# A gated mix of attention and a ReGLU block on one core: early weight loads merged in pairs, the last chunk of x moved to a later place, and the order of work laid out anew

## The chip, the cores and the metric

The kernel runs on one NeuronCore of one Trainium2 chip, as one program. The metric is the device time in microseconds of one execution; lower is better. All times of the trace are microseconds from the span's start, unless a row says ns.

## The reference

The input `x` has 2048 tokens of 512 numbers in bf16. Two branches work on it and a gate per token mixes them.

```python
g = sigmoid((x * gate_w).sum(-1, keepdims=True))
return g * A(x) + (1 - g) * B(x)
# B: three projections, D = 512, F = 1792
gate = x @ W_gate; up = x @ W_up
B = (gate * (gate > 0) * up) @ W_down
# A: 32 heads of 16, four segments of 512 tokens, a memory M, z carried from one to the next
for s in range(4):
    logits = qs @ ks.T * scale + mask      # mask: key after query
    a_dot = softmax(logits) @ vs
    a_mem = (phi(qs) @ M) / (phi(qs) @ z + 1e-6)
    o = sig(beta) * a_mem + (1 - sig(beta)) * a_dot
    M = M + phi(ks).T @ vs; z = z + phi(ks).sum(tokens)
A = o @ wo                                  # phi(t) = t + 1 if t > 0 else exp(t)
```

## The kernel before, in words

Everything is written out as a list of single steps, and each step goes to one engine's program in a fixed order. A step is a group of matmuls, one instruction of VectorE, ScalarE or GpSimd, or one transfer that SP issues. The string `ORDER` has one letter for each step to come; a letter stands for one of the queues that are made at the end of `program` (such as score blocks, exponentials, projections, the ReGLU block, the loads), and each letter takes that queue's next step. `BANKS` names the accumulator of each group in the same way. `Sched.place` derives the semaphore waits from what a step reads and writes. The numbers `occ`, `nbytes` and `after` given with a step are the planner's costs and due times; they went into the making of `ORDER` and set nothing on the chip. A transfer is tied to one of 16 semaphores, and an issue waits until the last transfer on its semaphore has landed.

Work is staged by four segments (chunks) of 512 tokens. For each there are:

- `proj` (L538 to L573): q, k and v by TensorE, in pairs of contraction tiles (`kt`, four of 128 rows), copied out by VectorE or ScalarE (L552, L556, L560, L573); masked copies `kp` of k (L564, L565); `phi` of q and k (L525 to L527), and a transpose of phi(k) by a transfer (L570, `phik`).
- `att` (L648): 18 score blocks ("quads") of a segment in the four banks `psL`, the exponential on ScalarE (L652), triangular masks on GpSimd (L657), then the product with v (L680, 64 matmuls a block), which also reads `vsh`, a copy of v shifted by 64 partitions (L630). VectorE transposes and scales the result (L690 to L707). The memory's part is L590 (update), L610 and L617 to L622 (use).
- `ffn` (L740): 14 slices of W_gate and W_up, the relu (L748, L749) and the product into `hT` (L751).
- `outp` (L772, L779): output of the segment before, scaled (L788, L789) and stored (L791).
- the token gate: rows of x are loaded into one buffer (L494, `ldxr4` to `ldxr15`), multiplied and summed by VectorE (L497, `gate4` to `gate15`), one after the other. The first four (L489) use the rows already loaded for chunk 0. `gexp` is written out and read back as `gexpT` (L505, L507).

The matmuls of score blocks, of L680 and L590 and of all the rest run in different array shapes, and TensorE runs its steps in order; so a step that waits holds all steps behind it. The ReGLU block and the output fill the time between score blocks.

All loads go through SP in the order of its letters: four pieces of x (chunk 0), `wq`, `wk`, `wv` in pieces of 128 rows, the first half (`load_gu(0)`) of W_gate and W_up in pieces of 128 rows and 896 columns, `braw` (beta), `gwb` (gate_w), the second half, then chunk 1 of x by four transposing transfers (L383). Chunks 2 and 3 of x and `wo` and W_down have queues of their own and stand where ORDER has put them. In the new file the lines up to this place are one less (L353 for L354).

Of the kernel before, what the change touches and what calls it, by code (L numbers as in the profile page):

```python
# [21 lines left out]

LETTERS = "abcdefghijklmnopqrstuvwxyzABCDEFGHIJKLMNOPQRSTUVWXYZ0123456789"
ORDER = (
    "gefafafefafefafefaefaggfgagggggahgihaisggsagggssaghgssigsahssissasbsssassssassssCassssBsasssCsasBabsasEsasHaEHsasyIaDpasaIwsIasDasaFsaysSIapsaFSwauIau"
    "FasLubSsIapjFSuwSukaunuLSuKSapnuwukuLSVuSLuVSuSndpKuwnuduLSuSuLSduKSkpRmuwkdsLSuSRsosBKSUsSsmREsnUSpJIsBlwusRuDUssxSLpSqUBSwSIsozsuzJSpSsDwSsdzSuIsBds"
    "KSpIsEQdswSQuuduFSsSLysScpzqFSwsPuzqcLToySzpTuSzwsSczuTsSFuTxuSLcsSLpSGsSzwsRszcBsuzsEpRswnUuuBSuSUIuKpIuzSwouSLsSsSLsSEQuuQKpsSRwuBSuuSLqKSRypuzSUSwu"
    "zuSUsLuzuSKnpuwsIoLSuSsDSuJSszpLSCuSwzsusQuLSuESnpKqzwSoszVsVzuGuSzuSyLpSszSwzsusFszuKSuSFpStnwLtSrtOumOSmopOStwSnWtItIuSrLtSpSOtOwSotOSMtqSWSpzswtXzs"
    "ztFrtSOpztOSwzttoOStSzWNSrtSOxpOSXtOStwIWtIsQttRxpSRswtBStSMsSuQXpntwAosQuuDSuStLSKqSRpUqPSRuUwzStTuzTUuTLuSpzKuTUnwtuzoSuzuuLKSpuSzwSuLStSuIuLJSpSsnw"
    "stAosBSsSuQEpSLtwSuSMuuXLuSqnLmSpmouSwzuSuzunsLSpuzSwLSuSsIosBuKSszuJzsEuLSSszuSCrApKuOOwuOuuLuLuSpSLqwuzVuVzuSKsSzpSzuwzsuSDuuLKSpzuSwSsAsLSWssFSpGrS"  # L30
    "ItwOSIttOStOStopSrWSwtSOtOtOtMWStSprXwuOtOtuOtxSLpWSqSwQtzSutzxSuSnpswsLSosSFtuzNSuIpJXLSuSwuzuQuLSuLsSpzGqwtnPSotzTqTQpzSuwTtzStSAttnptzSwouzzttSMTuz"
    "XStSKpAuwLSuStntuLSmpJSoIuwuSLtStSuStmSLrStOSunoNOpOuwuLuuXLruSOuOSKpOSuwSuLuqLSpSzuwSuzSuLuuzKSpzuwzuuLSSuzuSKpSAqwLSuzVuVzuSKpSzuwSzuLSuuzuKpSzuSwLu"
    "SuSAuuLWSuLSuKSuWSpLuwutLtStSrpSOtOwSuOtWtuSpLtSwttMtXSpuSwStSttqSSpSztwStzuztLtNSztzXtrSzuStOSOptOwtWuqLSpSzuwuztLuuzSpztwztMSSuAXuuzSKpStAwtSLtSuSuL"
    "SuSuKSuSpLuwuuLutLSuSuSuKSpuwuLtuqLSSpzuwuzuLuuzKSuzuzuuLSKSpzuSwuAtLuuLSuSvLSpuSwtuMuuLXSuSuLSvKSuvvuvLquzuzvKvzvzuzvuzvLvvAvvvvNvXNvvXvvvvvvNvvvXvvv"
    "vvvvNvvvvvXMX"
)
# [281 lines left out]
def program(sc, nc, T, PL, PA, A_x, A_wq, A_wk, A_wv, A_wo, A_beta, W_g, W_u, W_d, gate_w, out, NSEG, KT, NF, NT, EPS, SCALE):  # L318
    V = type("V", (), T)

    def op(eng, fn, occ, **k):
        return sc.add(Op([(eng, fn, occ)], **k))
# [30 lines left out]
    def load(eng, names, dst, src, nbytes, occ=460.0):  # L353
        (lact if eng == "act" else lsp).append(dma(eng, lambda e, dst=dst, src=src: e.dma_start(dst, src), nbytes, occ=occ, writes=names, name="ld" + names[0]))  # L354
    x0 = A_x[0, 0:512, :].rearrange("(i p) d -> p i d", p=128)
    def touch(n, src):
        load("act", ["adT"], V.adT[0:16, 32 * n:32 * n + 32], src, 1024)
    def load_x0(i):
        load("sp", [f"hT{i}"], V.hT[:, i, :], x0[:, i, :], 150000)

    def load_w(nm, w, src, kts):
        for kt in kts:
            load("sp", [f"{nm}{kt}"], w[:, kt, :], src[kt * 128:(kt + 1) * 128, :], 160000)
    load_x0(0)
    load_x0(1)
    load_w("wq", V.wq, A_wq, (0,))
    load_x0(2)
    load_x0(3)
# [12 lines left out]
    def load_x(c):
        for kt in range(KT):
            lsp.append(dma("sp", lambda e, c=c, kt=kt: e.dma_start_transpose(V.xT[:, kt, c * 512:(c + 1) * 512], A_x[0, c * 512:(c + 1) * 512, kt * 128:(kt + 1) * 128]),  # L383
                           1 << 17, occ=1280.0, writes=[f"xT{c}_{kt}"], name=f"ldx{c}_{kt}"))
# [57 lines left out]
    for h in range(2):  # L442
# [5 lines left out]
        for kt in range(KT):  # L448
            src, dst = PL[:, kt, 0:256], V.xT[:, kt, 256 * h:256 * h + 256]
# [78 lines left out]

    def proj(s):
        pes, evs, sbs, acts, sps = [], [], [], [], []  # L530
# [20 lines left out]
        def cp(fn, **k):  # L551
            return sc.add(Op([("dve", lambda e: fn(e, e.tensor_copy), t_dve(512)), ("act", lambda e: fn(e, lambda d, x: e.activation(d, x, ACT.Copy)), t_act(512))], **k))  # L552
        for G in range(4):
            ep = pj(V.wq, G, "q", "wq")
            qs = qslot(s, G)
            evs.append(cp(lambda e, f, ep=ep, qs=qs: f(V.qT[:, qs, :], A(ep)[:, :]), writes=[f"qT{qs}"], name=f"qcp{s}_{G}", ep=ep, role="r"))  # L556
            if s > 0 and G % 2:
                phi(s, "q", G, V.phiq, "phiq", V.qT, qs - 1, [f"qT{qs - 1}", f"qT{qs}"], acts, sbs)
            ep = pj(V.wk, G, "k", "wk")
            evs.append(cp(lambda e, f, ep=ep, G=G: f(V.kT[:, G, :], A(ep)[:, :]), writes=[f"kT{G}"], name=f"kcp{s}_{G}", ep=ep, role="r"))  # L560
            ks = kslot(s, G)
            kv = V.kT[:, G, :].rearrange("q (c k) -> q c k", c=8)
            for p in range(2):
                km = lambda e, kv=kv, p=p, ks=ks: e.tensor_scalar(V.kp[:, ks, :, 64 * p:64 * p + 64], kv, V.pm[:, p:p + 1], None, ALU.mult)  # L564
                ka = lambda e, kv=kv, p=p, ks=ks: e.activation(V.kp[:, ks, :, 64 * p:64 * p + 64], kv, ACT.Copy, scale=V.pm[:, p:p + 1])  # L565
                evs.append(sc.add(Op([("dve", km, 350)] + ([("act", ka, 720)] if s else []), reads=[f"kT{G}", "pm"], writes=[f"kp{ks}_{p}"], name=f"kmask{s}_{G}_{p}")))
            if s < NSEG - 1 and G % 2:
                phi(s, "k", G, V.ek, "ek", V.kT, G - 1, [f"kT{G - 1}", f"kT{G}"], acts, sbs)
                for g in (G - 1, G):
                    sps.append(dma("sp", lambda e, g=g: e.dma_start_transpose(V.phik[:, :, g * 128:(g + 1) * 128], V.ek[:, g, :]), 1 << 17, occ=1280.0, reads=[f"ek{g}"], writes=[f"phik{g}"], name=f"kT2{s}_{g}"))  # L570
# [320 lines left out]
```

## Time and profile before

| what | value |
|---|---|
| times of the runs | 265.28, 265.44 and 331.41 us; median 265.44 us |
| the profiled execution | 265.18 us, of it the span 263.2 us |
| TensorE busy | 259.5 us (99%), 2761 matmuls, clock 1.000 |
| VectorE busy | 189.3 us (72%), 365 instructions |
| ScalarE busy | 186.4 us (71%), 162 instructions |
| GpSimd busy | 124.7 us (47%), 283 instructions |
| transfers | 19.34 MB, mean 73 GB/s over the span |

The span goes from the first to the last instruction; the profiled execution's own time has 1.98 us more around it. The busy share of an engine is a mean over the whole span. The rows of a timeline give the start, the duration of the group, the engine (SPq is SP's queue of transfer issues), the line, the operation, the tiles written and read, the count and, in brackets, how long the engine stood idle before and what ended that. The row of a transfer issue lasts as long as SP is busy with it; when the data has landed is told by the view of transfers, as the median time from issue to landing.

### The profile page before, as it was taken

What the parts mean: (1) busy time and instruction counts of PE and PEld (TensorE: products, weight loads), DVE (VectorE), ACT (ScalarE), POOL (GpSimd) and SP (SyncE); (2) the same over time, 40 slices, a digit from 0 to 9 for tenths busy, and PEclk for the clock granted to TensorE, in tenths of its full rate; (3) what the DMA queues carried; (4) which work ended last, traced back from release to release, by engine and by line L of the source; (5) the groups of instructions that cost most, each with busy time, mean ns of one, the idle gap of its engine ahead of it and who ended that gap; (6) DMA issues with size and microseconds to landing.
All of it is one profiled execution on the core that took longest, in us unless ns stands there. A gap on an engine that the chain in (4) does not pass through costs nothing.

```text
span 263.2 us, 6640 instructions
## 1 busy us (share of the span) xinstructions
PE 259.5 (99%) x2761; PEld 115.2 (44%) x2761; DVE 189.3 (72%) x365; ACT 186.4 (71%) x162; POOL 124.7 (47%) x283
## 2 busy tenths in 40 slices
PE   8999999999999999999999999999999999999996
PEld 4644444334444444334444434444443443444444
DVE  5588887877887778888896779778854676485700
ACT  3688899888987694887686886868866567664021
POOL 3037456654645456755345467635554526334000
DMA  6889764693041222501032210110321010000011
GB/s 181 259 315 218 163 73 64 188 288 48 21 108 21 63 62 60 83 27 17 2 85 62 64 40 24 38 25 2 85 42 40 22 22 20 0 2 20 2 40 40
DMA packets 34684, 19.34 MB, mean 73 GB/s; under 512 B 24032, under 2 KB 34144, under 8 KB 34656
## 3 DMA queue, kind: packets, MB, share of 16 engines
q1 hardware_dynamic: 34560, 18.93, 31.0%
q8 instruction: 21, 0.34, 0.6%
q14 instruction: 7, 0.06, 0.1%
q10 hardware_dynamic: 96, 0.00, 0.0%
HBM read 9.87 MB, written 2.11 MB: 46 GB/s over the span
## 4 chain that ended last, share of the span: by engine, by line
PE 90%; SPq 4%; DVE 2%; DMA 2%; issue 0%; DVEq 0%
PE psA L740 35%; PE psA L779 19%; PE psL L648 8%; PE psA L547 7%; PE psA L680 6%; PE psA L772 5%; PE psA L545 4%; SPq L383 2%; DMA osb<-in_A_x_dram 2%; PE psA L538 2%; PE psA L610 1%; PE psL L437 1%; SPq L507 1%; SPq L570 1%; PE psL L446 1%; DVE Tn L690 0%
## 5 line engine op out<-in xcount | busy, mean ns | idle before, releaser
L657 POOL TENSOR_SCALAR_AFFINE_SELECT E<-E 64x256 bf16<-64x256 bf16 (+1 forms) x256 | 116.0, 464 | 114.6 <-ACT E L652 105.9
L652 ACT ACTIVATE E<-psL 128x2048 bf16<-128x2048 f32 x72 | 135.1, 1876 | 35.2 <-PE psL L648 32.9
L740 PE MATMUL psA<-xT,wu 128*128 128x512 bf16 x224 | 62.5, 380 | 0.0
L740 PE MATMUL psA<-xT,wg 128*128 128x512 bf16 x224 | 60.8, 380 | 0.0
L779 PE MATMUL psA<-wd,hT 128*128 128x512 bf16 (+2 forms) x238 | 59.3, 367 | 0.0
L751 DVE TENSOR_TENSOR hT<-psA,rl 128x512 bf16<-128x512 f32 x56 | 38.3, 687 | 14.6 <-PE psA L740 13.1
L779 PEld LDWEIGHTS psA<-wd,hT 128*128 128x128 bf16 x238 | 21.4, 98 | 24.1 <-issue 2.8
L740 PEld LDWEIGHTS psA<-xT,wg 128*128 128x128 bf16 x224 | 20.5, 98 | 25.3 <-issue 1.9
L740 PEld LDWEIGHTS psA<-xT,wu 128*128 128x128 bf16 x224 | 20.0, 98 | 25.6 <-issue 4.3
L690 DVE STREAM_TRANSPOSE Tn<-psA 128x512 f32<-128x512 f32 x32 | 21.0, 694 | 12.4 <-PE psA L680 12.4
L748 ACT ACTIVATE rl<-psA 128x512 bf16<-128x512 f32 x32 | 19.1, 596 | 14.5 <-PE psA L740 14.5
L648 PE MATMUL psL<-qT,kp 32*128 32x192 bf16 (+7 forms) x512 | 28.5, 287 | 0.0
L749 DVE TENSOR_SCALAR rl<-psA 128x512 bf16<-128x512 f32 x24 | 16.5, 688 | 6.8 <-PE psA L740 6.6
L648 PEld LDWEIGHTS psL<-qT,kp 32*128 32x128 bf16 x512 | 8.2, 92 | 26.3 <-issue 12.7
L680 PE MATMUL psA<-E,vaug 64*17 64x128 bf16 (+7 forms) x512 | 18.7, 283 | 0.0
L680 PE MATMUL psA<-E,vsh 64*17 64x128 bf16 (+7 forms) x512 | 18.3, 283 | 0.0
L547 PE MATMUL psA<-xT,wk 128*128 128x512 bf16 x64 | 17.1, 380 | 0.0
L545 PE MATMUL psA<-wv,xT 128*128 128x512 bf16 x64 | 16.8, 380 | 0.0
L772 PE MATMUL psA<-wo,oT 128*128 128x512 bf16 (+2 forms) x68 | 16.5, 367 | 0.0
L788 DVE TENSOR_SCALAR osb<-psA,omg 128x512 bf16<-128x512 f32 (+1 forms) x9 | 6.3, 705 | 13.6 <-PE psA L772 10.7
L680 PEld LDWEIGHTS psA<-E,vaug 64*17 64x17 bf16 x512 | 11.6, 86 | 7.8 <-issue 3.4
L789 ACT ACTIVATE osb<-psA,omg 128x512 bf16<-128x512 f32 (+1 forms) x8 | 5.4, 673 | 12.1 <-PE psA L772 10.7
(72 smaller groups left out, 237.0 us busy)
## 6 DMA issues: line engine op xcount, KB each, us to landing
vsh<-vaug SPq DMA_DIRECT2D x8, 272.0 KB, 3.7
out_dram<-osb SPq DMA_DIRECT2D x15, 128.0 KB, 1.7
wg<-in_B_W_gate_dram SPq DMA_DIRECT2D x8, 224.0 KB, 6.4
wu<-in_B_W_up_dram SPq DMA_DIRECT2D x8, 224.0 KB, 6.0
wd<-in_B_W_down_dram SPq DMA_DIRECT2D x3, 512.0 KB, 6.4
osb<-in_A_x_dram SPq DMA_DIRECT2D x12, 128.0 KB, 2.2
hT<-in_A_x_dram SPq DMA_DIRECT2D x4, 128.0 KB, 2.2
wq<-in_A_wq_dram SPq DMA_DIRECT2D x4, 128.0 KB, 2.8
```

What stands on the lines that cost most here:

```text
L545: ins = e.matmul(A(ep)[:, :], lhsT=V.xT[:, kt, tok + col * 128:tok + (col + 1) * 128], rhs=w[:, kt, :], start=(kt == 0), stop=(kt == KT - 1))
L547: ins = e.matmul(A(ep)[:, :], lhsT=w[:, kt, col * 128:(col + 1) * 128], rhs=V.xT[:, kt, tok:tok + 512], start=(kt == 0), stop=(kt == KT - 1))
L648: ins = q.matmul(PL[:, jj, o:o + 512 - 64 * c], lhsT=V.kp[r, kslot(s, G), c, :], rhs=V.qT[r, qslot(s, G), 64 * c:512], start=True, stop=Tr ...
L652: acts.append(act(lambda a: a.activation(V.E[:, e, :, :], PL[:, :, :], ACT.Exp, scale=SCALE), t_act(2048), reads=[f"bankL{b}" for b in ran ...
L657: pools.append(pool(lambda g, ap=ap, base=base: g.affine_select(out=ap, in_=ap, compare_op=ALU.is_ge, fill=0.0, base=base, pattern=[[0, 4] ...
L680: ins = q.matmul(A(eps[p])[32 * jj:32 * jj + 17, 64 * c:512], lhsT=v[:, 8 * G + 2 * jj + p, :], rhs=V.E[r, e, jj, o:o + 512 - 64 * c], sta ...
L690: ds.append(dve(lambda e, p=p, ep=eps[p]: e.transpose(V.Tn[:, p, :], A(ep)[:, :]), 706, writes=[f"Tn{p}"], name=f"tr{s}_{G}_{p}", ep=eps[p ...
L740: ins = e.matmul(A(ep)[:, :], lhsT=w[:, kt, f * 128:(f + 1) * 128], rhs=V.xT[:, kt, c * 512:(c + 1) * 512], start=(kt == 0), stop=(kt == K ...
L748: evs.append(sc.add(Op([("act", lambda e, ep=eg, r=r: e.activation(V.rl[:, r, :], A(ep)[:, :], ACT.Relu), t_act(512)), ("dve", lambda e, e ...
L751: evs.append(dve(lambda e, ep=eu, r=r, hs=hs: e.tensor_tensor(V.hT[:, hs, :], A(ep)[:, :], V.rl[:, r, :], ALU.mult), t_dve(512), reads=[f" ...
L772: ins = e.matmul(A(ep)[:, 0:c1 - c0], lhsT=V.oT[:, o0 + G, i * 128:(i + 1) * 128], rhs=V.wo[:, G, c0:c1], start=st_ and G == 0, stop=sp_ a ...
L779: ins = e.matmul(A(ep)[:, 0:c1 - c0], lhsT=V.hT[:, slots[f], i * 128:(i + 1) * 128], rhs=V.wd[:, f, c0:c1], start=st_ and f == f0, stop=sp ...
```

## The change

The merged loads, and the place of the last chunk:

```diff
-    def load_x0(i):
-        load("sp", [f"hT{i}"], V.hT[:, i, :], x0[:, i, :], 150000)
-
-    def load_w(nm, w, src, kts):
-        for kt in kts:
-            load("sp", [f"{nm}{kt}"], w[:, kt, :], src[kt * 128:(kt + 1) * 128, :], 160000)
...
-    load_w("wq", V.wq, A_wq, (1, 2, 3))
-    load_w("wk", V.wk, A_wk, range(KT))
-    load_w("wv", V.wv, A_wv, range(KT))
+    def load_x0(i, nb):
+        load("sp", [f"hT{i}"], V.hT[:, i, :], x0[:, i, :], nb)
+
+    def load_w(nm, w, src, k0, k1, nb, a=0, b=512, tag=""):
+        load("sp", [f"{nm}{tag}{kt}" for kt in range(k0, k1)], w[:, k0:k1, a:b], src[k0 * 128:k1 * 128, a:b].rearrange("(k p) c -> p k c", p=128), nb)
...
+    load_w("wq", V.wq, A_wq, 1, 2, 250000)
+    load_w("wq", V.wq, A_wq, 2, 4, 280000)
+    load_w("wk", V.wk, A_wk, 0, 2, 440000)
+    load_w("wk", V.wk, A_wk, 2, 4, 280000)
+    load_w("wv", V.wv, A_wv, 0, 4, 780000)
...
-            for kt in range(KT):
-                load("sp", [f"{nm}{h}_{kt}"], w[:, kt, a:b], src[kt * 128:(kt + 1) * 128, a:b], 256 * (b - a) + (748000 if (nm, h, kt) == ("wg", 0, 0) else 0))
+            for kt in (0, 2):
+                load_w(nm, w, src, kt, kt + 2, 410000 + (200000 if (nm, h) == ("wg", 0) else 0), a, b, f"{h}_")
...
-                           1 << 17, occ=1280.0, writes=[f"xT{c}_{kt}"], name=f"ldx{c}_{kt}"))
+                           1 << 17, occ=1350.0, writes=[f"xT{c}_{kt}"], name=f"ldx{c}_{kt}"))
...
-    load("sp", ["braw"], V.braw[:], A_beta.partition_broadcast(128), 8192)
-    load("sp", ["gwb"], V.gwb[:], gate_w.partition_broadcast(128), 400000)
+    load("sp", ["braw"], V.braw[:], A_beta.partition_broadcast(128), 300000, occ=670.0)
+    load("sp", ["gwb"], V.gwb[:], gate_w.partition_broadcast(128), 500000)
...
-            t.after = 22000.0 + 14000.0 * (c - 2)
+            t.after = (24000.0, 100000.0)[c - 2]
```

The planner's cost of a phik transpose goes from 1280 to 1450. `ORDER` (1499 letters, 1513 before, for 14 loads fewer) and `BANKS` are other strings: the same steps in another order and in other accumulators, and for steps that two engines can do, another choice between VectorE and ScalarE in some places. What follows from that on SP: 20 loads stand ahead of chunk 1 where there were 34; two phik transposes now come between chunk 1 and `vsh`; chunk 3, which stood ahead of `wo`, now stands behind the third store of segment 0 and the load `ldxr9`, with two phik transposes between its third and its fourth piece.

More of the change, by code (lines that the diff above doesn't have):

```diff
@@ L24 @@
 ORDER = (
[L25 to L32, printed above, removed]
@@ L33 @@
-    "SuSAuuLWSuLSuKSuWSpLuwutLtStSrpSOtOwSuOtWtuSpLtSwttMtXSpuSwStSttqSSpSztwStzuztLtNSztzXtrSzuStOSOptOwtWuqLSpSzuwuztLuuzSpztwztMSSuAXuuzSKpStAwtSLtSuSuL"
-    "SuSuKSuSpLuwuuLutLSuSuSuKSpuwuLtuqLSSpzuwuzuLuuzKSuzuzuuLSKSpzuSwuAtLuuLSuSvLSpuSwtuMuuLXSuSuLSvKSuvvuvLquzuzvKvzvzuzvuzvLvvAvvvvNvXNvvXvvvvvvNvvvXvvv"
-    "vvvvNvvvvvXMX"
+    "gefafafefafefafefaefaggfgagggggahgihaigagggggsashsisggasshissassbssassssassssssasCssssaBssssCassBasasEassHEHsasyIDpsIwsaIsDuFsaysSIsFSubpIsKIsRwuFuRuu"
+    "LUjSuKkpnuwUksLSuSuFuSKSpnVuwVuLSuSunduKpnuwLSduSukSsLSudblkpmsLSwSsdRsBuSSsoDmpSsSnwIuBSsuLsJSuRqELSUxSpIswzSuUuzssLoCuSIsyzuSDpSsSwLsIsBusIxsQpDSuSw"
@@ new lines @@
+    "QsucFsSuSLypSszLScuwouFqzqcPKSzTpuSzwSuzTscSuLTuzSsKRpscFSwuSzuRusLSUuSGzpsKUIswIunuBSosSuLTsSpzEuSQwuLSuSsQssLCSpSsRwsDSssRqCnUyQpuzSUwSszSssSDuozuSK"
+    "zpszwsBSuSuDSuJSzpuSwLSuSuLuIuLKSuSpynqLwouVzuVuzsKSzpSszwszuFSuSsLSpGuSzwSsLtSnrsOmStOmoGpSOtSwnWtSIsIsrFtSpSOtOwSotOSttMSpWtSwttXrtOtOSpOSuwSWtStqMo"
+    "SXpSztwSzStItzrItxOSpztOSztwtOuStSzWtxSMSpqQXwtPunuLTouKSudRtLSqSdApRtwdzStTuzTuUTunKpuwzSuUQtLSuSuzdKpQuwIuoLSuSuIuLSpStzwutLSuSMuSKpSnXuwuLsSouSzqSK"
+    "SRpzSuwSszSuBsuLSsSuzEnpuKIsIwuAuzLSuSszKssCRsmDSsUmsSCzSrsSOUpnEOuAwuOuouLuLuSpQqwLSuzVuVzsSKuSozpSzswzuuBSusLKSpzuSwSsAuDSWssLSpGrSItwOSIttOStOStWpS"
@@ new lines @@
+    "tSwrStoOtOtONSWtSprwtXOuOtOutWxSLpSqSwQuzSttzxSsSnptwtIoMStSzXtIuzQpuLSwsSzutFSuKSunutLSoqSzptwPtAtQqMTSpXTztSwzStTnusKztSozuzupSztTwLuSsSAutFSKtSntum"
+    "SpmouSnwIuLSuuIuLSptLSwSuMSuosLrsSOuOSGpOXuwuLuuLruSOpOSuLwSuSOuuLqSLSpSzuwSuzuLuuzSuLSuKzpzuwuSzuSLuuLSpqSAwLuVzuVuSKzuSpSzuLwSuzuzuuLSpzuSwSuLSuAuLu"
+    "WSpKLuSSwuWStLuuSrKtSOStOtSOptwWtuurLtSpSOtOwtOMtWtSpqSXwSStzuztSuSzpSKztzwttSztMtStAXpStwStStuqSSpztwtztMuzXSpztwzuuLSSuLuSpSztSwLuStSAutLSuSuSuLSuuK"
+    "upLuwuuLtuSpLuSwSuSuLtuSuLSpuwuLuuLtSuNSuLSuXSuLpqwuzuLuSpSzvwSvLSuzuzuzKuSuzuSLuSKuSAvqLvzvzvvzuzvzuuzKuAvLvvvvvvvNvXNvvXvvvvvvNvvvXvvvvvvvNvvvvvXMX"
@@ L36 @@
 )
 BANKS = (
-    "012312301230123012301320132013201320312032012031023123013201320130231023102301313120101312302302302320323201320132012012301230132030203013013023021010"
-    "21313012012301230123012301230131230302012012320320320320320320321321321310"
+    "012312301230132032013201320123012310231032102310213201320123013021320123012310212120231223130130130130123013021302302301230123012013101201230130320313"
+    "01301301201230123012301203120320202013013232012012012012013203120120120203"
 )
@@ L357, in touch @@
         load("act", ["adT"], V.adT[0:16, 32 * n:32 * n + 32], src, 1024)
-    def load_x0(i):
-        load("sp", [f"hT{i}"], V.hT[:, i, :], x0[:, i, :], 150000)
-    def load_w(nm, w, src, kts):
-        for kt in kts:
-            load("sp", [f"{nm}{kt}"], w[:, kt, :], src[kt * 128:(kt + 1) * 128, :], 160000)
[L364 to L368, printed above, removed]
-    load_w("wq", V.wq, A_wq, (1, 2, 3))
-    load_w("wk", V.wk, A_wk, range(KT))
-    load_w("wv", V.wv, A_wv, range(KT))
+    def load_x0(i, nb):
+        load("sp", [f"hT{i}"], V.hT[:, i, :], x0[:, i, :], nb)
+    def load_w(nm, w, src, k0, k1, nb, a=0, b=512, tag=""):
+        load("sp", [f"{nm}{tag}{kt}" for kt in range(k0, k1)], w[:, k0:k1, a:b], src[k0 * 128:k1 * 128, a:b].rearrange("(k p) c -> p k c", p=128), nb)
+    load_x0(0, 150000)
+    load_x0(1, 150000)
+    load_w("wq", V.wq, A_wq, 0, 1, 250000)
+    load_x0(2, 130000)
+    load_x0(3, 130000)
+    load_w("wq", V.wq, A_wq, 1, 2, 250000)
[3 more added lines that the diff above has]
+    load_w("wv", V.wv, A_wv, 0, 4, 780000)
     half = (NF // 2) * 128
@@ L569, in proj @@
                 for g in (G - 1, G):
-                    sps.append(dma("sp", lambda e, g=g: e.dma_start_transpose(V.phik[:, :, g * 128:(g + 1) * 128], V.ek[:, g, :]), 1 << 17, occ=1280.0, reads=[f"ek{g}"], writes=[f"phik{g}"], name=f"kT2{s}_{g}"))
+                    sps.append(dma("sp", lambda e, g=g: e.dma_start_transpose(V.phik[:, :, g * 128:(g + 1) * 128], V.ek[:, g, :]), 1 << 17, occ=1450.0, reads=[f"ek{g}"], writes=[f"phik{g}"], name=f"kT2{s}_{g}"))
         for tt in range(4):
```

## The prediction

> **What bounds the kernel now.** I read the page's totals first, then the waits of TensorE, then the timeline round the one wait, last the queue that issues the transfers.
>
> ```profile
> span 263.2 us, 6640 instructions
> PE 259.5 (99%) x2761; PEld 115.2 (44%) x2761; DVE 189.3 (72%) x365; ACT 186.4 (71%) x162; POOL 124.7 (47%) x283
> ...
> 13.36 2.16 PE psA L545 x10
> ...
> PE psL L437 <- PEq L876: 0.8, 1, 0.8
> PE psA L547 <- DVE hT L751: 0.4, 1, 0.4
> ```
>
> TensorE is busy for 99% of the span, and its waits name only the start and one stall. A busy figure can hide gaps, since the ends are modelled, so I laid the matmuls of the old order end to end: 0.216 us for each of 512 columns (the chain's row: ten in 2.16). With 0.43 us for a score block, 1.10 for a block of L680 and the change-over before it, the sum meets the starts of all score blocks in the trace within 0.1 us, once two things are added: some 1.3 us in the head, and one step of 0.6 us near 57 us. So after the head the old kernel loses 0.6 us in all. The rest is work.
>
> ```profile
> 56.22 1.03 PE L547 MATMUL psA<-xT,wk 128*128 128x512 bf16 x4
> 57.67 0.60 PE L547 MATMUL psA<-xT,wq 128*128 128x512 bf16 x2 [0.42 <-DVE hT L751]
> ...
> 54.42 0.69 DVE L497 CUSTOM_DVE_ANT_0 osb<-osb,gwb 128x512 bf16<-128x512 bf16 x1 [1.56 <-DMA osb<-in_A_x_dram]
> ...
> 56.97 1.24 DVE L751 TENSOR_TENSOR hT<-psA,rl 128x512 bf16<-128x512 f32 x2
> ...
> 42.03 5.79 SPq L383 DMA_TRANSPOSE xT<-in_A_x_dram  x4
> 47.86 0.58 SPq L354 DMA_DIRECT2D wo<-in_A_wo_dram  x1
> 48.49 0.51 SPq L354 DMA_DIRECT2D wd<-in_B_W_down_dram  x1
> 49.04 1.08 SPq L494 DMA_DIRECT2D osb<-in_A_x_dram  x1
> ...
> osb<-in_A_x_dram SPq DMA_DIRECT2D x1, 128.0 KB, 5.4
> ```
>
> The step's cause: four matmuls from 56.22 end their turn at 57.08 (4 x 0.216) and the next starts at 57.67: 0.59 us. It waited for an accumulator that the product of L751 at 56.97 frees. That product was late because VectorE stood 1.56 us before the first gate product (L497, "gate4"), whose rows of x were issued at 49.04 and took 5.4 us. They were issued late because the four transposes of chunk 3 of x held SP for 5.79 us at 42.03.
>
> **The change part by part.** The order of instructions shows the same matmuls in the same counts, 601 planned TensorE steps and 164 change-overs between kinds of matmul on both sides. So TensorE's work is unchanged, and the change can only remove the head and the 0.6 us, or add waits. More than about 2 us (0.7%) isn't there to be won.
>
> *Chunk 3 moves.* Its transposes leave the place at 42 us; in the new SP order gate4's rows come right after wo and one piece of wd. From the rows below, SP comes to it near 42.3: 24.3 at the end of chunk 1, two phik transposes of 1.69, vsh 1.23, chunk 2 6.13, a small store, two phik, four gexpT reads 2.00, wo and wd. Landing 5.4 us later it is there at 47.7, and gate4 now stands behind one more product, wanted after 53 us. The stall goes: -0.6 us (bounds -0.6 and 0: 0 if another VectorE wait of that size comes instead). What hid the old place cost nothing else. At its new place three transposes follow the gate row "gate9", and the fourth follows two phik transposes.
>
> *Merged loads.* Fourteen of 34 early issues on SP go. Merged issues cost 0.5 to 0.6 us (wo and wd above) against 0.46, so SP alone would win some 5 us. It won't get them:
>
> ```profile
> 3.14 1.38 SPq L354 DMA_DIRECT2D wq<-in_A_wq_dram  x3
> 8.36 1.85 SPq L354 DMA_DIRECT2D wg<-in_B_W_gate_dram  x4
> 12.16 0.67 SPq L354 DMA_DIRECT2D braw<-in_A_beta_dram  x1
> 14.81 1.22 SPq L354 DMA_DIRECT2D wg<-in_B_W_gate_dram  x1
> 19.68 5.33 SPq L383 DMA_TRANSPOSE xT<-in_A_x_dram  x4
> 25.05 1.23 SPq L630 DMA_DIRECT2D vsh<-vaug  x2
> 26.32 6.13 SPq L383 DMA_TRANSPOSE xT<-in_A_x_dram  x4
> 33.18 6.75 SPq L570 DMA_TRANSPOSE phik<-ek  x4
> 39.99 2.00 SPq L507 DMA_DIRECT2D gexpT<-gscr  x4
> ...
> 2.00:12.00 10.00, 10.00 (x66) 6.36 (x65) 4.78 (x13) 4.03 (x10) 1.05 (x5) 1.00 0.89 257
> 12.00:22.00 10.00, 10.00 (x68) 3.85 (x67) 8.32 (x18) 8.54 (x8) 3.48 (x9) 1.00 0.96 319
> ...
> braw<-in_A_beta_dram SPq DMA_DIRECT2D x1, 8.0 KB, 6.6
> ```
>
> The DMA engines are 89% and 96% busy in those stretches (last two columns: share, GB/s), so bytes, not issues, set the landings. At 14.81 an issue of 0.46 stretches to 1.22 us: SP is held by what is still outstanding. Chunk 1's issue began at 19.68, some 0.9 us after braw (issued at 12.16, landing 6.6 us later: 18.8); at that moment gwb and eight weight pieces were outstanding. I take it that the same amount may be outstanding after the change, so SP comes to chunk 1 when braw has landed, sooner only by the idle DMA time that closes: at most 11% of 10 us and 4% of 7, 1.4 us; I take half, 0.7, thus 19.0 (bounds 18.3 and 19.68).
>
> The Trainium skill ("Trace Analysis", section "DMA Instruction — HWDGE (DVE, Sync)") says that an issue's row ends when its descriptors are generated, and that the engines start early where these don't fit the buffer. The stretched 1.22 agrees; the sum is the same with or without it. Its page "DMA: Bandwidth & Descriptors" ("Rules for kernel authors") would coalesce for bandwidth, and its fit of 2 us and 436 GB/s would, as an estimate, bring the 5.8 MB of weights and x in by about 16 us instead of 25; then the new wait below would be nothing, and the sum 0.3 us lower. The 257 GB/s at a busy share of 0.89 speaks against it.
>
> *Weights in time?* A merged load serves only when its last byte is in:
>
> ```profile
> wq<-in_A_wq_dram SPq DMA_DIRECT2D x1, 128.0 KB, 2.7
> wg<-in_B_W_gate_dram SPq DMA_DIRECT2D x1, 224.0 KB, 5.0
> wu<-in_B_W_up_dram SPq DMA_DIRECT2D x4, 224.0 KB, 5.3
> ...
> 16.22 1.03 PE L740 MATMUL psA<-xT,wg 128*128 128x512 bf16 x4
> 17.52 0.59 PE L740 MATMUL psA<-xT,wu 128*128 128x512 bf16 x2
> 27.89 0.59 PE L547 MATMUL psA<-xT,wq 128*128 128x512 bf16 x2
> 34.36 0.39 PE L680 MATMUL psA<-E,vaug 64*17 64x512 bf16 x4
> ```
>
> The old fourth wg piece (issued 9.75) landed at 14.75 and the fourth wu piece (11.7) near 17.0. In the new order the first wg pair is used five matmul pairs earlier (14.06), its second at 15.8, wu at 17.5 and 18.0: all after the old landings, and the byte queue is not slower. Cost 0. The head: the last three wq rows come as one and two; the old fourth landed at 4.08+2.7=6.8, and its turn is now near 7.4. All sixteen transposes of x by TensorE now stand before most of the wq products; 28 run unbroken where 26 did. I take -0.15 us (bounds -0.4 if nothing is waited for, +0.9 if the pair needs as long as wo, below).
>
> *A new wait.* The first use of chunk 1 (27.89) stands three pairs earlier, 1.3 us, and with the head it is wanted at 26.4. The last transpose of chunk 1 was issued 3.86 us after the first and landed 3.8 us after that (next fence). From 19.0 it lands at 26.7: 0.3 us late. Bounds: 0 (SP at 18.3) to 1.0 (SP at 19.68 as before). Behind it TensorE waits whole. vsh now stands behind two phik transposes (3.4 us): second issue 28.4, landing 4.2 later, 32.6; the first L680 block is wanted at 33.0 (34.36 less 1.2 and the head), so 0, and later still if chunk 1 is late.
>
> ```profile
> 23.54 1.46 SPq L383 DMA_TRANSPOSE xT<-in_A_x_dram  x1
> ...
> xT<-in_A_x_dram SPq DMA_TRANSPOSE x1, 3.8
> ...
> vsh<-vaug SPq DMA_DIRECT2D x1, 272.0 KB, 4.2
> ...
> wo<-in_A_wo_dram SPq DMA_DIRECT2D x1, 512.0 KB, 4.7
> ...
> L652 ACT ACTIVATE E<-psL 128x2048 bf16<-128x2048 f32 x72 | 135.1, 1876 | 35.2 <-PE psL L648 32.9
> ```
>
> *The rest of the new order.* VectorE gets seven instructions more and ScalarE seven fewer (masks, copies, outputs; by the totals a VectorE instruction is 189.3/365, 0.52 us): some 4 us more in 263, hidden behind TensorE as long as VectorE is at 72 to 74%. Score blocks stay at least 2.26 us of matmuls apart, against an exponential of 1.876; 22 stand at that distance where 16 did without a wait. Cost 0; if the cover goes, 0.1 us each.
>
> The sum against the profiled execution (263.2 in the span, 265.18 in all): 263.2 - 0.6 - 0.15 + 0.3 = 262.75, and 1.98 round it, 264.7. The median of the runs shown, 265.44, lies 0.26 above the profiled one and the lowest 0.1; I add 0.2: **264.9**.
>
> **The rivals.** *Chunk 1 late in full*: SP is held to 19.68 whatever is merged, the head gains nothing, and chunk 1 costs 1.0 us. For it: the stretched issues. Against: DMA shares under 1. 265.38 - 0.6 + 1.0 = 265.8; 0.18. *The stall moves*: another VectorE instruction waits for its rows of x, gate9 above all, which follows its load's release by 3.8 us of matmuls where old gates had 4.4 or more. 264.9 + 0.6 = 265.5; 0.10. *The other side, chunk 3 late*: its last transpose is queued on SP behind two phik transposes that wait for VectorE, and everything on TensorE stands behind the first wq product of that chunk.
>
> ```profile
> 103.45 5.89 SPq L570 DMA_TRANSPOSE phik<-ek  x4
> ...
> xT<-in_A_x_dram SPq DMA_TRANSPOSE x1, 4.3
> ```
>
> The phik pair can go near 103.5, as before; with 1.47 each the last x transpose goes at 106.5 and lands at 110.8. Laid end to end, the new order wants it at 114.4. It decides once VectorE is 3.6 us late there; at 6 us late it would cost 2.4: 267.3, slower than before; 0.06. The skill's same rules say to issue a transfer early and wait late, which speaks against this move; by that the sum would be this rival's. *Merged loads run at the lone pace of wo*: 512 KB in 4.7 us, 112 GB/s. The 3.14 MB from the third wq piece to the end of wu would land at 34 instead of 17, and chunk 1, behind 1.97 MB more, at 52 instead of 26.4: about 290. It passes 2% below some 200 GB/s. Against: wo was issued straight behind four transposes, so its 4.7 us holds their time too; 0.03. *All of it fits*: the bytes come faster in larger pieces, as the skill's rule would have it, and chunk 1 is early: 264.9 - 0.3 = 264.6; 0.10.
>
> **How the numbers follow.** Forecast 0.53. Its range is 264.1 (full head gain, no wait) to 265.6; the rivals within 1% reach 264.6, 265.8 and 267.3, and the head may cost 0.9 where I have a gain, so the range is 264.0 to 266.8. A measurement of this kernel tells about 2% from no change. Slower by more: 0.04 (the lone pace, and a share of the late chunk 3). Faster by more would need TensorE's work to shrink: 0.01. Within: 0.95.
>
> **What would show it.** Right: no TensorE wait near 57 us, gate4 without a DMA wait, its rows issued near 42; SP at chunk 1 near 19 with stretched issues from 7 us on; a wait under 0.6 us before the first wq product of chunk 1; score blocks after it at constant distance from the laid-out sum. Wrong: a TensorE wait over 1 us anywhere, SP at chunk 1 before 15 us, or a step near 114 us.

## The result and the profile after

The changed kernel took 269.42 us at the median of 13 runs (267.35 to 270.95), the kernel before 265.44 beside it. The ratio is 1.0133 (95% interval 1.0097 to 1.0169): 1.3% slower, where the prediction had 264.9 us and a range up to 266.8. The profiled execution took 269.52 us, 267.8 of it the span, 4.6 us more than the span before.

The page of the changed kernel, its totals and the granted clock in 40 slices of 6.7 us:

```profile
span 267.8 us, 6584 instructions
PE 255.7 (95%) x2725; PEld 114.8 (43%) x2761; DVE 190.8 (71%) x372; ACT 182.1 (68%) x155; POOL 124.5 (46%) x283
...
PEclk9999999889999999999999999999999999999999
```

Of 2761 weight loads 2725 have their matmul on record; the 36 missing ones leave false gaps of 0.16 us "<-issue" in the views below. Not false is the dip of the clock in slices 8 and 9. The waits of TensorE (line and what it waited for: total us, times, longest):

```profile
PE psA L740 <- issue: 4.7, 15, 2.5
...
PE psL L437 <- PEq L876: 0.8, 1, 0.8
PE psA L538 <- DMA wq<-in_A_wq_dram: 0.5, 1, 0.5
PE psL L446 <- DMA hT<-in_A_x_dram: 0.5, 2, 0.3
```

The old wait for the product of L751 is gone, and two short waits for the first loads are new. The longest is 2.5 us for "issue": TensorE waited for no semaphore. The timeline shows where:

```profile
45.81 0.66 PE L590 MATMUL psA<-vaug,phik 128*32 128x34 bf16 x63
46.40 0.39 PE L680 MATMUL psA<-E,vaug 64*17 64x512 bf16 x4
46.42 0.57 PE L680 MATMUL psA<-E,vsh 64*17 64x512 bf16 x8
...
47.37 0.20 PE L680 MATMUL psA<-E,vaug 64*17 64x64 bf16 x4
47.50 0.40 PE L648 MATMUL psL<-qT,kp 32*128 32x256 bf16 x8
48.06 0.38 PE L740 MATMUL psA<-xT,wu 128*128 128x512 bf16 x1 [0.16 <-issue]
50.92 0.59 PE L740 MATMUL psA<-xT,wu 128*128 128x512 bf16 x2 [2.48 <-issue]
51.35 0.90 PE L545 MATMUL psA<-wv,xT 128*128 128x512 bf16 x2
52.04 1.91 PE L740 MATMUL psA<-xT,wg 128*128 128x512 bf16 x4
```

Three things are to be seen. The update block (L590) and a product block (L680) stand back to back: 128 short matmuls, each with a weight load, in 1.8 us. Then TensorE stands for 2.48 us. Then it works at half pace: four matmuls of 512 columns take 1.91 us instead of 1.03. The clock record gives a granted clock of 0.5 from 51.50 us for 3.41 us and 1.0 on both sides. Of the 13 runs six had a mean clock of 0.993 or 0.994 (mean 270.1 us) and seven one of 0.998 or more (268.3).

What SP issued meanwhile (start, time that SP was held, operation):

```profile
12.62 11.92 SPq L383 DMA_TRANSPOSE xT<-in_A_x_dram  x4
...
40.33 0.43 SPq L353 DMA_DIRECT2D wo<-in_A_wo_dram  x1
40.80 0.51 SPq L353 DMA_DIRECT2D wd<-in_B_W_down_dram  x1
41.35 0.51 SPq L494 DMA_DIRECT2D osb<-in_A_x_dram  x1
41.91 1.61 SPq L353 DMA_DIRECT2D wd<-in_B_W_down_dram  x3
```

wo and W_down, 2.4 MB, now leave at 40.3 to 43.5 us, 7.5 us earlier than before, mostly because chunk 3 (5.79 us of SP) no longer stands ahead of them. These five loads are called the bulk below. The transfers of 44 to 48 us, then those of 48 to 50 (packets, MB, share of the 16 engines; a packet counts in the window where it starts, so a share can pass 100%):

```profile
DMA packets 1452, 1.44 MB, mean 360 GB/s; under 512 B 51, under 2 KB 1451, under 8 KB 1451
q1 hardware_dynamic: 1451, 1.43, 108.3%
...
q8 instruction: 1, 0.02, 3.5%
```

The bulk has all the transfer engines. And there is a second queue, q8, for instructions: 21 blocks of 16 KB in the whole span, one for some 260 of TensorE's 5522 matmuls and weight loads. I read them as TensorE's own code, which experiment 7 puts to the test, as does a count behind the experiments. The one in the second window starts at 48.50 us and takes 1.11. TensorE goes on 1.31 us after it is in. In the kernel before, the block at that place came at 44.20, ahead of the bulk.

Added up from the starts of the score blocks against the laid-out sum, in us, changed minus before: head +0.1, chunk 1 +0.2, the step at 48 to 54 us +4.2 (2.5 of standing, 1.7 of half clock), gate 4's stall -0.6; the last store +0.6 (below). That is 4.5 of the 4.6.

### The profile page after: what moved, and what is told of

Its sections match the earlier page's. It is cut to its first block, busy times and chain, and to the rows that moved or that the text cites. A ratio compares the mean times of both kernels' runs of the same rounds, so it can differ in the third digit from the quotient of the medians.

```text
span 267.8 us, 6584 instructions
## 1 busy us (share of the span) xinstructions
PE 255.7 (95%) x2725; PEld 114.8 (43%) x2761; DVE 190.8 (71%) x372; ACT 182.1 (68%) x155; POOL 124.5 (46%) x283
## 4 chain that ended last, share of the span: by engine, by line
PE 93%; issue 3%; DMA 1%; SPq 1%; ACT 1%; DVE 0%; DVEq 0%
PE psA L740 37%; PE psA L779 18%; PE psA L547 9%; PE psL L648 9%; PE psA L680 6%; PE psA L545 6%; PE psA L772 5%; DMA wq<-in_A_wq_dram 1%; PE psA L610 1%; SPq L353 1%; PE psA L538 1%; PE psA L590 1%; ACT ek L525 0%; ACT qT L552 0%; DVE osb L788 0%
## 5 line engine op out<-in xcount | busy, mean ns | idle before, releaser
L740 PE MATMUL psA<-xT,wu 128*128 128x512 bf16 x218 | 60.4, 380 | 3.4 <-issue 3.4
L740 PE MATMUL psA<-xT,wg 128*128 128x512 bf16 x210 | 59.0, 384 | 1.7 <-issue 1.3
L779 PE MATMUL psA<-wd,hT 128*128 128x512 bf16 (+2 forms) x229 | 56.7, 367 | 1.3 <-issue 1.3
L751 DVE TENSOR_TENSOR hT<-psA,rl 128x512 bf16<-128x512 f32 x56 | 38.4, 685 | 16.0 <-PE psA L740 15.3
L779 PEld LDWEIGHTS psA<-wd,hT 128*128 128x128 bf16 x238 | 20.7, 98 | 23.4 <-issue 3.9
L748 ACT ACTIVATE rl<-psA 128x512 bf16<-128x512 f32 x31 | 18.5, 596 | 17.4 <-PE psA L740 17.3
L749 DVE TENSOR_SCALAR rl<-psA 128x512 bf16<-128x512 f32 x25 | 17.2, 686 | 4.7 <-PE psA L740 4.6
L680 PE MATMUL psA<-E,vaug 64*17 64x128 bf16 (+7 forms) x512 | 18.7, 283 | 0.0
L545 PE MATMUL psA<-wv,xT 128*128 128x512 bf16 x63 | 18.5, 393 | 0.2 <-issue 0.2
L680 PE MATMUL psA<-E,vsh 64*17 64x128 bf16 (+7 forms) x512 | 18.3, 283 | 0.0
L788 DVE TENSOR_SCALAR osb<-psA,omg 128x512 bf16<-128x512 f32 (+1 forms) x11 | 7.8, 710 | 14.7 <-PE psA L772 11.4
L772 PE MATMUL psA<-wo,oT 128*128 128x512 bf16 (+2 forms) x64 | 15.6, 366 | 0.4 <-issue 0.3
L680 PEld LDWEIGHTS psA<-E,vaug 64*17 64x17 bf16 x512 | 11.6, 86 | 7.4 <-issue 3.6
L547 PE MATMUL psA<-xT,wq 128*128 128x512 bf16 x47 | 13.1, 380 | 0.2 <-issue 0.2
```

The source lines that it names most:

```text
L545: ins = e.matmul(A(ep)[:, :], lhsT=V.xT[:, kt, tok + col * 128:tok + (col + 1) * 128], rhs=w[:, kt, :], start=(kt == 0), stop=(kt == KT - 1))
L547: ins = e.matmul(A(ep)[:, :], lhsT=w[:, kt, col * 128:(col + 1) * 128], rhs=V.xT[:, kt, tok:tok + 512], start=(kt == 0), stop=(kt == KT - 1))
L680: ins = q.matmul(A(eps[p])[32 * jj:32 * jj + 17, 64 * c:512], lhsT=v[:, 8 * G + 2 * jj + p, :], rhs=V.E[r, e, jj, o:o + 512 - 64 * c], sta ...
L740: ins = e.matmul(A(ep)[:, :], lhsT=w[:, kt, f * 128:(f + 1) * 128], rhs=V.xT[:, kt, c * 512:(c + 1) * 512], start=(kt == 0), stop=(kt == K ...
L748: evs.append(sc.add(Op([("act", lambda e, ep=eg, r=r: e.activation(V.rl[:, r, :], A(ep)[:, :], ACT.Relu), t_act(512)), ("dve", lambda e, e ...
L751: evs.append(dve(lambda e, ep=eu, r=r, hs=hs: e.tensor_tensor(V.hT[:, hs, :], A(ep)[:, :], V.rl[:, r, :], ALU.mult), t_dve(512), reads=[f" ...
```

## The experiments

The theory: *TensorE's next code block is asked for ahead of the dense stretch, waits behind the bulk, and comes after the stretch has eaten the block in hand.* Rivals: the dense stretch outruns the code whatever the bulk does; any code block under a bulk stalls TensorE, dense stretch or not; the merged loads or the new order are the cause. Steps are named in SP's order below: grd0 is the read of gexpT, rows4 the x rows of gate 4, phik1_0 the transpose of phik's tile 0 in segment 1. The profile shows one execution of each kernel; the ratio is over all its runs, against the kernel before on the same chip.

**1. The bulk late, all else as changed.**

```diff
-grd0 wo wd0 rows4 wd4 wd8 wd12 phik1_0 phik1_1 rows5
+grd0 rows4 phik1_0 phik1_1 wo wd0 rows5 wd4 wd8 wd12
```

> The changed kernel with one thing put back: wo and the first W_down load leave SP only behind the transpose of phik's tile 1 of segment 1, and the other three W_down loads behind the rows of gate 5, as late as the bulk went in the kernel before; chunk 3 of x stays far behind, and TensorE's order is untouched. Theory (the bulk load is ahead of TensorE's code in the transfers just where update block L590 and product block L680 stand back to back): the 2.5 us gap at 50.9 and the half clock behind it are gone, span about 263.6, time about 265.3, the same as before within 0.3 us. First rival (the dense stretch alone outruns the code, bulk or not): the gap stays, span about 267.8, time about 269.5. Second rival (a code block under any bulk load stalls, dense stretch or not): the gap moves to the later bulk, 1 to 4 us near 50 to 56, time 267 to 270.

Measured: 266.27 us, ratio 1.0046 (1.0020 to 1.0073), span 264.7: 1 us more than expected. But the gap and the half clock are gone; the code block came at 46.59, 0.2 us ahead of L590. That rules out the dense stretch alone. Nor did the later bulk stall anything, though here neither a dense stretch nor a code block met it (the blocks near it came at 49.92 and 65.21). What is left over lies in the first 28 us and behind the last matmul.

**2. The bulk early in the old order.**

```diff
 in the kernel before:
-grd0 x3_0 x3_1 x3_2 x3_3 wo wd0 rows4 wd4 wd8 wd12
+grd0 wo wd0 rows4 wd4 wd8 wd12 x3_0 x3_1 x3_2 x3_3
```

> The kernel before with one thing changed: the four transposes of chunk 3 of x move behind the last W_down load, so that wo and W_down go about 6 us earlier, at about 42 to 51 us, as in the changed kernel, but in the old order of TensorE's work, where update block and product block stand four projections apart. Theory (bulk and a dense stretch are both needed): no gap of TensorE over 0.3 us between 42 and 52, the 0.64 us wait of gate 4 at 57 gone, span about 262.6, time about 264.6, 0.3% below before. Second rival (bulk alone holds the code up): a gap of 1 to 4 us near 46 to 51 with a half clock behind it, time 267 to 269. Chunk 3 late would show as a wait before the first wq product of segment 3.

Measured: 266.23 us, ratio 1.0043 (1.0018 to 1.0068), span 265.0. My expectation failed: a gap as in the changed kernel, in the old order and with single loads.

```profile
47.12 0.38 PE L740 MATMUL psA<-xT,wu 128*128 128x512 bf16 x1
49.71 0.38 PE L740 MATMUL psA<-xT,wu 128*128 128x512 bf16 x1 [2.21 <-issue]
```

So neither the new order nor the merging is needed; the early bulk is enough. That four projections stand between L590 and L680 in the old order doesn't help: both together still use up about one block. The clock stayed at 1.0 here.

**3. Chunk 3 back ahead of wo.**

```diff
-grd0 wo wd0 rows4 wd4 wd8 wd12
+grd0 x3_0 x3_1 x3_2 x3_3 wo wd0 rows4 wd4 wd8 wd12
```

> The changed kernel with chunk 3 of x put back ahead of wo, right behind chunk 2: the merged loads and the new order of all engines stay. Theory: wo and W_down are issued near 46 to 48 and the dense stretch at 46 to 48 has its code; the step of 4.2 us is gone or under 1, span 263.2 to 264.5 (the 0.6 us wait of gate 4 may come back), time 265 to 266.4. Third rival (the merged loads or the new order cause the step wherever chunk 3 stands): the step stays at 4, time about 269.5.

Measured: 265.98 us, ratio 1.0029 (1.0004 to 1.0054), span 264.6. wo left at 45.74, the code block came at 47.16, and the step shrank from 4.2 to 0.6 us:

```profile
49.37 0.59 PE L740 MATMUL psA<-xT,wu 128*128 128x512 bf16 x2 [0.45 <-issue]
```

The third rival falls.

**4. The merged loads alone**, with the old order and chunk 3 at its old place.

```diff
 the load code of the changed kernel, with
-ORDER, BANKS of the changed kernel
+ORDER of the kernel before less the 14 issues merged away, its BANKS
-            t.after = (24000.0, 100000.0)[c - 2]
+            t.after = 22000.0 + 14000.0 * (c - 2)
```

> The merged early weight loads alone: the changed kernel's loads with the old order of work and chunk 3 at its old place. Theory: merging costs and gains nothing that counts; span 262.9 to 263.6, time about 265.3, the 0.64 us wait of gate 4 stays, and no code gap appears. Third rival (the merged loads are what costs): time 267 to 269.5, with gaps in the first 30 us.

Measured: 267.00 us, ratio 1.0064 (1.0035 to 1.0094). That they cost nothing was wrong, and so was it that the wait of gate 4 stays: that step of 0.6 us is gone here, and the kernel is slower all the same. In this profile the first score block stands 3.4 us behind the laid-out sum instead of 1.3. TensorE waited 0.46 for hT, 0.35 and 0.58 for wq, and then here for a wk product:

```profile
14.57 0.39 PE L648 MATMUL psL<-qT,kp 32*128 32x512 bf16 x4 [1.18 <-DVE kp L564]
```

With the other profiles, that head offset is 0.9 to 1.3 in the four kernels with single loads (before, 2, 8, 9) and 1.3 to 3.4 in the eight with merged ones. It changes from run to run: this kernel's runs go from 265.13 to 268.33, and the two slowest had a mean clock of 0.994, for which no trace was kept.

**5. Half of the bulk early.**

```diff
-grd0 wo wd0 rows4 wd4 wd8 wd12 phik1_0 phik1_1 rows5
+grd0 wo wd0 rows4 phik1_0 phik1_1 rows5 wd4 wd8 wd12
```

> The changed kernel with only part of the bulk early: wo and the first W_down load stay at 40.3 us, the other three W_down loads (1.3 MB) go behind the rows of gate 5. At the 370 GB/s of the changed kernel's bulk the remaining 1.15 MB are through near 45.5, before TensorE's code block is asked for (about 45.7, just ahead of update block L590). Theory (the code block stands in the queue behind the bulk): no gap over 0.4 us between 46 and 53, span 264 to 264.8, time about 266. Rival (any bulk issued before the dense stretch stalls it): a gap near 2.5, time near 269.

Measured: 265.52 us, ratio 1.0029 (1.0008 to 1.0051), span 263.5. No gap; the code block came at 45.44, 0.3 us ahead of L590, with the stretch as dense as before. wo left at 39.18 in this execution.

**6. More bulk**, a copy of W_down into a scratch in the chip's memory.

```diff
-grd0 wo wd0 rows4 wd4 wd8 wd12 phik1_0
+grd0 wo wd0 rows4 wd4 wd8 wd12 copy0 copy4 copy8 copy12 phik1_0
```

> The changed kernel with 1.84 MB more behind the last W_down load: W_down is copied once more, into a scratch in the chip's memory that nothing reads. Theory (the code block waits for what was issued ahead of it): 1.84 MB at 370 GB/s are 5 us more, the code block comes near 53.5 and not 48.5, the gap of TensorE grows from 2.5 to about 7.5 us, span 272 to 274. Rival (the stall has a fixed price, or the code shares the transfer engines in turn): the gap stays at 2.5 to 3.5, span 268 to 269.

Measured: 269.08 us (two runs only), ratio 1.0158 (1.0116 to 1.0201), span 267.5. The prediction of 7.5 us was wrong; the gap stayed:

```profile
50.48 1.01 PE L745 MATMUL psA<-xT,wu 128*128 128x512 bf16 x2 [2.31 <-issue]
```

```profile
43.60 6.54 SPq L354 DMA_DIRECT2D scr<-in_B_W_down_dram  x4
```

The transfer engines were full until 53.5 us, yet the code block came at 48.08. SP was held for 6.54 us in issuing the copies: they left at 43.60, 44.62, 45.99 and 47.44. A free block would have come near 45.3 (L590 is at 45.54; see the table below). Two copies had left ahead of that and landed at 52.59 and 53.88, and the block was in at 49.21. So the block doesn't wait for all that was issued ahead of it, at most for what is under way at its request.

**7. The code shifted, transfers and order untouched.**

```diff
-xps, xcs = [warm(5, 512, 0, 3)], []
+xps, xcs = [warm(69, 32, 0, 3)], []
```

> The changed kernel with its transfers and its order of work untouched, but 64 more small matmuls at its very start: the warm-up is 69 matmuls of 32 columns instead of 5 of 512 (what they compute is not used). Each brings a weight load, so all later code of TensorE stands 128 instructions (8 KB) further back, and the edge of a 16 KB code block that falls just ahead of the dense stretch at 45.8 us falls about 6 us earlier, before the bulk. Theory: no gap over 0.4 us between 46 and 53 although the bulk and the dense stretch meet as before; apart from what the warm-up adds at the head (0 to 1.5 us), span 264 to 264.8. Rival (the bulk slows TensorE's work there in another way): the gap of about 2.5 stays, span near 268.

Measured: 265.52 us, ratio 1.0023 (0.9991 to 1.0055), span 263.6. The windows of this kernel (length; PE, PEld, DVE, ACT, POOL busy, granted clock, transfer share, GB/s):

```profile
42.00:48.00 6.00, 6.00 (x161) 2.98 (x160) 5.06 (x10) 5.08 (x4) 3.37 (x8) 1.00 0.93 295
48.00:54.00 6.00, 6.00 (x41) 2.37 (x41) 5.12 (x10) 5.06 (x5) 4.66 (x10) 1.00 0.50 146
```

```profile
41.03 0.43 SPq L353 DMA_DIRECT2D wo<-in_A_wo_dram  x1
```

The same bulk at the same time, the same dense stretch (L590 at 45.87), and TensorE busy throughout. The code blocks came at 35.73 and 50.20: one before the bulk, the next within it, when the block in hand still lasted. So a code block under the bulk does not stall TensorE by itself, which answers the second rival. Apart from the small matmuls at the very start, only where the edge of a block falls was changed, so this is the run that shows the cause to be the code.

**8. The old order with late bulk and later chunk 3**, to take the one gain without the price.

```diff
 in the kernel before:
-grd0 x3_0 x3_1 x3_2 x3_3 wo wd0 rows4 wd4 wd8 wd12 phik1_0 phik1_1 rows5 phik1_2 phik1_3 rows6
+grd0 rows4 phik1_0 phik1_1 wo wd0 rows5 wd4 wd8 wd12 phik1_2 phik1_3 rows6 x3_0 x3_1 x3_2 x3_3
```

> The kernel before, order of work and single loads untouched, but wo and the first W_down load go behind the transpose of phik's tile 1 of segment 1, the other W_down loads behind the rows of gate 5, and chunk 3 of x behind the rows of gate 6, so that the rows of gate 4 leave SP near 42 without a bulk anywhere near the dense stretch. Theory: the 0.64 us wait at 57 is gone and no code gap takes its place: span about 262.6, time about 264.8, 0.2 to 0.3% below before. Rivals: W_down or chunk 3 late (a wait before the first product that reads them, time over 266), or a code gap at the later bulk (1 to 3 us near 55 to 65).

Measured: 264.42 us (264.24 to 264.75, 12 runs), ratio 0.9979 (0.9962 to 0.9995). Of the kernels here it alone has its whole interval below the one before.

```profile
span 262.4 us, 6640 instructions
PE 258.5 (99%) x2761; PEld 115.0 (44%) x2761; DVE 189.5 (72%) x365; ACT 186.4 (71%) x162; POOL 125.8 (48%) x283
```

```profile
40.60 1.13 SPq L494 DMA_DIRECT2D osb<-in_A_x_dram  x1
...
55.25 0.58 SPq L354 DMA_DIRECT2D wo<-in_A_wo_dram  x1
```

After the head, no score block moves against the laid-out sum by more than 0.08 us. Gate 4's rows left at 40.60, and its stall is gone.

**9. The new order alone**, with single loads and the bulk late.

```diff
 the load code of the kernel before, with
-ORDER, BANKS of the kernel before
+ORDER of experiment 1 with the 14 issues put back, BANKS of the changed kernel
```

> The new order of work alone: its chunk 3 at 105 us and its order on all engines, but the early weights loaded tile by tile as before, and wo and W_down late as in the first experiment, so that no code gap is in the way. In the runs so far the first score block stood 1.0 to 1.3 us behind the laid-out sum with single loads (three kernels) and 1.4 to 3.4 with merged ones (six). Theory: the single loads give the old head, about 1.2, but hold SP to 19.7 at chunk 1, so that its first wq product waits 0 to 1.0 us; no gate 4 wait and no code gap; span 262.4 to 263.6, time 264.4 to 265.6. Rival (the merged loads save more at chunk 1 than they cost at the head): a wait over 1 us at 26 to 28 us, time 266 to 267.

Measured: 265.91 us, ratio 1.0008 (0.9979 to 1.0036), span 264.3. The head is 0.9, and chunk 1 is late for its first product, as the prediction's first rival had it, by half a microsecond and not one:

```profile
18.53 6.09 SPq L383 DMA_TRANSPOSE xT<-in_A_x_dram  x4
```

```profile
26.93 0.59 PE L547 MATMUL psA<-xT,wq 128*128 128x512 bf16 x2 [0.49 <-DMA xT<-in_A_x_dram]
```

Against the expectation, a gap is there at 48 us with no bulk near:

```profile
48.16 0.28 PE L648 MATMUL psL<-qT,kp 32*128 32x256 bf16 x2 [0.24 <-issue]
```

The score blocks behind it start 0.5 us later against those ahead of it than in experiment 5. The code block came at 45.60, was in at 46.81, and TensorE went on at 48.16. So in the new order the block is only just in time even alone.

**10. The bulk in half-size pieces**, at the same place.

```diff
-    load("sp", ["wo"], V.wo[:], A_wo.rearrange("(g p) n -> p g n", p=128), 1 << 19)
+    for g in (0, 2):
+        load("sp", [f"wo{g}"], V.wo[:, g:g + 2, :], A_wo[g * 128:g * 128 + 256, :].rearrange("(g p) n -> p g n", p=128), 1 << 18)
...
-    for f0 in range(0, NF, 4):
-        f1 = min(f0 + 4, NF)
+    for f0 in range(0, NF, 2):
+        f1 = min(f0 + 2, NF)
```

> The changed kernel with the same bulk at the same place, but in pieces of half the size: wo as two loads of 256 KB and W_down as seven of 256 KB, nine issues from 40.3 to some 45 us instead of five until 43.5. So far the code block came 2.8 to 3.3 us late in three kernels with the full bulk, and no later when 1.84 MB more stood behind it, so it does not wait for all that is queued. Theory of the queue (it waits for what is under way at its request, some 1.3 MB either way): block at 48 to 48.5, gap 2 to 2.5, span 267 to 268. Theory of the turn (it waits for a turn whose length goes by the size of one load's share on a transfer engine, 32 pieces of 1 KB at 0.044 us for 512 KB, or two such shares): block late by half as much, 1.4 us, gap 0.5 to 1.1, span 264.5 to 266, time 266 to 267.5.

Measured: 267.18 us (265.16 to 268.49), ratio 1.0061 (1.0030 to 1.0093), span 266.0.

```profile
45.74 0.67 PE L592 MATMUL psA<-vaug,phik 128*32 128x34 bf16 x64
...
50.58 0.59 PE L742 MATMUL psA<-xT,wu 128*128 128x512 bf16 x2 [2.20 <-issue]
```

The code block came at 48.22, as late as with whole loads, and the gap is of the queue's size; the theory of a turn by the size of a load falls. The clock stayed at 1.0, which is why the span is below the 267 expected. The spans of its runs, 263.4 to 266.8, suggest that the gap isn't there in all of them.

## Why the prediction was wrong

What the cause rests on, in one table: the start of L590, the code block at that place, when it was in, and when TensorE went on after the gap (us).

| kernel | bulk from | L590 | block came | in | TensorE on | after "in" |
|---|---|---|---|---|---|---|
| changed | 40.33 | 45.81 | 48.50 | 49.61 | 50.92 | 1.31 |
| 6, more bulk | 40.22 | 45.54 | 48.08 | 49.21 | 50.48 | 1.27 |
| 10, half pieces | 39.97 | 45.74 | 48.22 | 49.27 | 50.58 | 1.31 |
| 3, chunk 3 ahead | 45.74 | 46.30 | 47.16 | 48.11 | 49.37 | 1.26 |
| 9, single loads, bulk late | 55.17 | 45.84 | 45.60 | 46.81 | 48.16 | 1.35 |
| 5, half early | 39.18 | 45.75 | 45.44 | 46.37 | no gap | |
| 1, bulk late | 55.62 | 46.79 | 46.59 | 47.54 | no gap | |
| 2, old order, bulk early | 41.51 | 43.25 | 47.31 | 48.38 | 49.71 | 1.33 |
| before | 47.86 | 43.24 | 44.20 | 45.45 | no gap | |
| 8, old order, bulk late | 55.25 | 43.05 | 43.78 | 44.93 | no gap | |

In the new order a free block comes 0.2 to 0.3 us before L590, in the old one 0.7 to 1.0 after it. Under the full bulk it comes 2.5 to 2.7 and 4.1 after it: about 3 us late each time. In experiment 3, where the bulk had only just begun, it comes 0.9 after it, some 1.1 us late. And each of the six gaps ends 1.26 to 1.35 us after the block is in.

A count shows the same. Up to the gap, TensorE has gone through 962 instructions in each of the six kernels, counting from the trace every weight load, a matmul for each and the semaphore instructions: in the changed kernel and in experiments 3, 6 and 10, 474 weight loads and 14 semaphore instructions; in experiment 2, with another order of work, 471 and 20; in experiment 9, 470 and 22. So the place is fixed in the code and not in the work. In experiment 7 the same count falls inside the block of L680, at 46.50, and nothing waits there.

By the prediction's own steps:

- *Chunk 3 moves.* The gain was right: gate 4's rows left at 41.35 (42.3 said), the stall is gone, and experiment 8 has that gain alone, 0.2%. The step that failed is its sentence that what hid the old place cost nothing else. With it 2.4 MB of loads left 7.5 us earlier, and I priced what the move brings forward only for gate 4's rows. wo and W_down I took as harmless because nothing needed them sooner or later; what they would run into I did not ask. Missing term: +4.2 in the profiled run.
- *Merged loads.* The head was to gain 0.15; it lost 0.1 in the profile of the changed kernel, 0 to 2.1 over all kernels with merged loads, and alone they cost 0.6% in the old order: the upper bound of +0.9 was too low. SP reached chunk 1 at 12.62, which the prediction named as a sign against it; it was not held until braw had landed (17.56), but by the four transposes themselves, for 11.92 us. The fit of 2 us and 436 GB/s that the prediction took from the Trainium skill ("DMA: Bandwidth & Descriptors") is given there for transfers that GpSimd issues; these go through SP.
- *A new wait.* 0.2 us before the first wq product of chunk 1, 0.3 said. The last transpose landed at 26.77, 26.7 said. That the transfers and not SP's issues set the landing was right; but SP was held elsewhere than said, so that the number came this near is in part luck.
- *The rest of the new order*, said to cost 0: the sum after the head holds within 0.1 us in experiments 5 and 7. But all eight kernels with the new order take 3.4 to 3.7 us from the start of their last matmuls to the end of the span, the four with the old order 2.8; their last store lands 2.1 to 2.3 us after its issue and not 1.4 to 1.5. That is 0.6 to 0.9 us that the prediction had not. In all eight, and in none of the four, an instruction block of 8 KB on another queue, q14, starts 0.7 to 1.0 us after that store's issue (at 265.93 in the changed kernel, the store at 265.25). No run tried whether that holds the store back.
- *Chunk 3 late*: no wait. Its last piece left at 112.40, landed at 115.20 and was first read at 119.05, where the sum had 106.5, 110.8 and 114.4: all later, the step of 4.2 us ahead of them included, with 3.9 us to spare and not 3.6.
- *The laid-out sum* could see waits for data and for buffers. A wait for code stands in no semaphore, so none of the rivals, nor the range, contained it. Two slips in the range bear on nothing here: its inner lower end of 264.1 is 264.35 by its own terms, and the rival at 267.3 lies above its upper end of 266.8.

In ratios: without the gap, or with the short one of experiment 3, the changed kernel stands at 1.002 to 1.005 (experiments 1, 3, 5 and 7), with it at 1.013, so about 1% is the code gap with its half clock. What is left above 1 is about what merging, chunk 1 and the last store cost beyond the 0.6 us gained; these runs don't part them further.

How the block waits is not settled. Experiment 6 rules out a wait for all that was issued ahead, experiment 10 one that goes by the size of a load. What is under way at the request would fit both, but was not varied by itself. On its own queue the block should wait for one turn only by the Trainium skill ("DMA: Bandwidth & Descriptors", section "Queues, rings and completion order": an engine changes queues between packets, of at most 64 descriptors). By that ceiling and the 0.044 us for 1 KB that 1452 packets in 4 us on 16 engines give, I estimate 2.8 us, near the 3 measured, if a packet of the profile is one descriptor; by the 9 to 17 descriptors that the same page of the Trainium skill calls typical it would be 0.4 to 0.75 us. No run here shows how many an engine took in one turn.

## What to carry to other kernels

Moving a transfer out of a queue moves everything behind it forward: price the bulk that it releases as well, and look at what else uses the transfer engines at its new time. An engine's code is one of those users; where many short instructions stand together, count them in blocks of some 260, and keep the large loads that nobody waits for away from the place where the next block comes. A gap "<-issue" with no semaphore behind it, just after a dense stretch, is the sign to look at the instruction queue.

## What the runs showed of the hardware

- TensorE's code arrives during the run in 16 KB blocks on a queue of its own, over the same transfer engines as the loads. A block takes 0.9 to 1.7 us as a rule, serves 1.3 us after it is in, and came about 3 us late under loads of some 360 GB/s.
- Where a block's edge falls decides whether that is felt: the six gaps all begin behind TensorE's 962nd instruction by the count above, in two orders of work, and 128 more instructions at the start took the gap away and gave back 1%.
- With a gap of 2.48 or 2.31 us the granted clock fell to 0.5 for 3.41 us, beginning 3.1 or 2.1 us after TensorE had stopped (changed kernel, experiment 6: there 0.2 us before it went on); with gaps of 2.2 (experiments 2 and 10) it did not. The Trainium skill ("TensorE: Matmul & The Clock Gate", section "What's actually happening") has windows of 3413 ns that run freely and half rate after at least one idle window. The length agrees; here less than a window of standing was enough.
